# Clustered attention and routed experts on one core: the first expert turn's weight sums moved from VectorE to GpSimd, and its preparation placed at other steps

## The chip, the cores and the metric

The kernel runs on one core of a Trainium2 chip. The metric is the device time of one execution in microseconds. A core has five engines with a queue each: TensorE (PE; its weight loads are shown apart as PEld), VectorE (DVE), ScalarE (ACT), GpSimd (POOL) and SyncE (SP), which issues most of the transfers here. An engine works its queue in order; a semaphore holds an instruction until what it needs is there, and everything queued behind it waits too.

## The reference

Two blocks follow each other. The first is an attention in which a query sees only the keys of its own cluster:

```
q_assign = argmax(einsum('bhsd,hcd->bhsc', q_n, c_n))      # 16 clusters per head
k_assign = argmax(einsum('bhsd,hcd->bhsc', k_n, c_n))
mask     = q_assign[..., :, None] == k_assign[..., None, :]
scores   = where(mask, q @ k.T / sqrt(64), -1e9)
attn_out = softmax(scores) @ v                             # (4, 8, 768, 64)
```

Its output, as 3072 rows of 512, goes into a layer of 8 experts of which each row uses one:

```
logits     = x @ w_gate                                    # (3072, 8)
expert_idx = argmax(logits)
gate_w     = softmax(logits)[expert_idx]
y[rows of e] = relu(x[rows of e] @ w1[e]) @ w2[e]          # w1: 512x1024, w2: 1024x512
out        = gate_w * y
```

All is float32.

## The kernel before

**Attention.** The 32 heads (4 batches of 8) are worked as 16 pairs, numbered 0 to 15, four to a batch. A pair has two halves (h) of six key blocks (j). For each of the 12 steps TensorE computes scores of both heads into PSUM (L433: a float32 product of q and k, then a bf16 product of the masks mq and mk that pushes foreign clusters down), ScalarE takes the exponential (L445, tile A), and VectorE adds A into acc (L451), the softmax's denominators. After the 12 steps TensorE multiplies all A by v (L457), which takes about 8 us. The denominators of pair n are summed by TensorE early in pair n+1 (sum_up, L480, 12 products that need the last acc of pair n) and worked on by VectorE (weights_of, from L489).

**Preparation of a pair.** While pair n runs, pair n+1 is prepared: VectorE transposes q and k into qT and kT (L277), TensorE multiplies them by the centroids (L291), VectorE finds the best cluster (assign0 to assign2: L302, L309, L311, L318, L320, L322, and L327, which ends in ohT), and ScalarE scales the result into mk (L340) and mq (L337).

**Order of the work.** A list written out by hand says after which step each piece of other work is emitted: `at_pair(n, u, f)` puts f after step u of pair n, where u = 0 to 11 are the score steps, 12 is between the two halves of the product with v, and 13 is after it. `between(n, u)` (L868) calls what is listed. Each engine's queue follows from that list.

**Experts.** The rows are handled in ten turns, called slots. Slots 0 and 1 (288 rows each) take rows of the first three batches only, so that they can be prepared during the last batch, pairs 12 to 15; slot 0 is computed when attention has ended. The steps that prepare it:

- `number` (L598 to L607): VectorE computes each token's place and GpSimd writes the tokens to DRAM (tokens_of) by indirect transfers.
- `rank_first` (L642): 13 small VectorE instructions that pick the experts of slots 0 and 1 and write them, with offsets, to xe.
- `first_turns` (L849): SP loads the numbers from xe into registers (expert, places), fetches the token lists sf from DRAM (L712, L716), and then the expert's weights w1 (L97) and w2 (L105), 2048 KB each.
- `indices` (L722): VectorE turns sf into row numbers gi and si (L728, L729).
- `gather` (L731): GpSimd fetches the rows xg by indirect transfers (L738), three for a slot of 288 rows.
- `weigh` (L744): VectorE multiplies the rows by the softmax weights into xw (L755) and SP stores them in DRAM (turn_rows, L761).
- `take` (L765): SP loads them back as xs (L771) in the layout that VectorE's transpose needs.
- `turn_rows` (L776): VectorE transposes xs into xT (L780).
- `x_sums` (L791) and `w1_sums` (L809): the sums of one step of Strassen's scheme, four of xT's blocks (tile xc) and four of w1's (tiles a0 to a3, 128 x 1024 float32 each). Both are issued by `strassen` (L788), so they share line 789.

`layer1` (L947) then multiplies w1 and the rows with seven products per half instead of eight (L968). Its order of use for the weight sums is a2, a1, a0, a3. Between its products, hooks run the rest of pair 15: sum_up in hook 2, weights_of, gate and others behind it.

In w1_sums the sums depend on one another as follows:

```
0: lambda: (a21, a22, ALU.add), 1: lambda: (a22, A[2], ALU.subtract),
2: lambda: (a11, a21, ALU.subtract), 3: lambda: (a12, A[1], ALU.subtract),
```

Of the kernel before, what the change touches and what calls it, by code (L numbers as in the profile page):

```python
# [33 lines left out]
def kernel(  # L34
# [11 lines left out]
    nc = tc.nc  # L46
# [121 lines left out]
    with tc.manual_schedule(), ExitStack() as actx:  # L168
# [655 lines left out]
        def at_pair(n, u, f, *a):  # L824
            AT.setdefault((n, u), []).append(lambda: f(*a))
# [8 lines left out]
        for b in range(B - 1):  # L834
            n = HP * (b + 1)
# [8 lines left out]
            at_pair(n, 2, weights_of, n - 1)  # L844
        n = HP * (B - 1)
        slots = range(len(EARLY))
        at_pair(n + 1, 4, rank_first)

        def first_turns():  # L849
            for s in slots:  # L850
# [3 lines left out]
            GR[0]["w1"] = fetch1(GR[0]["e"], wa)  # L854
            GR[0]["w2"] = fetch2(GR[0]["e"], wa)

        at_pair(n + 1, 6, first_turns)
        for s in slots:
            at_pair(n + 1, 13, indices, s)
        at_pair(n + 2, 6, gather, 0)  # L860
        at_pair(n + 2, 13, weigh, 0)
        at_pair(n + 3, 1, take, 0)
        at_pair(n + 3, 4, turn_rows, 0)
        at_pair(n + 3, 6, x_sums, 0)
        at_pair(n + 3, 9, w1_sums, 0, (2, 1), nc.vector)
        at_pair(n + 3, 13, w1_sums, 0, (0, 3), nc.vector)

        def between(n, u):  # L868
            for f in AT.pop((n, u), ()):
# [24 lines left out]
    with tc.manual_schedule(), ExitStack() as ectx:  # L894
# [262 lines left out]
        n = NPAIR  # L1157
# [357 lines left out]
```

## Time and profile before

| | |
|---|---|
| runs | 660.57, 660.47, 659.32 us; median 660.47 |
| profiled execution | 659.27 us, of which the span from first to last instruction is 657.5 |
| granted TensorE clock | 0.998 |
| pair 13 (TensorE's first score to the next pair's) | 268.96 to 288.84, 19.88 us |
| pair 14 | 288.84 to 310.37, 21.53 us |
| pair 15 | 310.37 to 329.47, 19.10 us; no preparation of a next pair in it |
| slot 0, layer 1 | 329.47 to 347.20 |
| rank_first on VectorE | 279.60 to 281.86 |
| issue of w1 and w2 of slot 0 | 290.39 and 290.92; on their way 7.4 and 16.1 us |
| gathers on GpSimd (slot 0's three, slot 1's first) | start 293.49, 294.79, 296.83, 298.02 |
| slot 1's other two gathers | 311.75 and 313.09 |
| xw of slot 0 on VectorE | 310.36 to 313.63 |
| xT of slot 0 on VectorE | 322.41, after 2.48 us of waiting for xs |
| weight sums of slot 0 on VectorE | 329.26 to 331.75 and 333.59 to 335.95 |

In the profile's text a line has, in this order: source line, engine, operation, the tile written and the tiles read, size and number, then busy time and the mean of one instruction in ns, and at the end the idle time before and what ended it. A line in order of time starts with its start and its length in us; what stands in brackets is how long the engine stood idle before it and which instruction released it. A row of the table by stretch has start and end, its length, then busy us and number of instructions for PE, PEld, DVE, ACT and POOL, the granted clock, the share of the DMA engines that was busy, and GB/s. Times in all views count from the span's start.

### The profile page before, as it was taken

To read this page: it belongs to the slowest core of one execution; us is meant where nothing else is said; L and a number is where in the kernel's file an instruction comes from. 1 tells how busy PE (TensorE), PEld (TensorE's weight loads), DVE (VectorE), ACT (ScalarE), POOL (GpSimd) and SP (SyncE) were. 2 spreads that over 40 slices of the span, in tenths; PEclk is the share of its full clock that TensorE was granted. 3 is DMA by queue.
4 is the path that set the end of the run, shared out by engine and by line. 5 is a ranking of instruction groups with operands and counts; after the bars stand their busy time and mean duration, and the time that the engine had idled before them with its cause. 6 is when DMAs were issued, how large, how long until landed. Compare 5 with 4: busy or idle time off the path is not lost.

```text
span 657.5 us, 11491 instructions
## 1 busy us (share of the span) xinstructions
PE 644.2 (98%) x4252; PEld 423.3 (64%) x4252; DVE 490.0 (75%) x845; ACT 338.8 (52%) x584; POOL 130.8 (20%) x166
## 2 busy tenths in 40 slices
PE   8999999999999999999999999999999999999996
PEld 4444544455444454544484979989797987869773
DVE  6988888998889988989887997888869365572300
ACT  4677878768878777867532333333231331323210
POOL 4500000022000300041103522324240422140010
PEclk9999999999999999999999999999999999999999
DMA  7663455443355433347475587776684835614010
GB/s 150 150 120 68 76 94 97 72 80 68 73 97 98 74 76 72 72 132 227 117 273 156 187 314 264 252 275 211 249 307 170 273 138 165 233 74 173 7 49 19
DMA packets 189760, 95.38 MB, mean 145 GB/s; under 512 B 152895, under 2 KB 171839, under 8 KB 188416
## 3 DMA queue, kind: packets, MB, share of 16 engines
q1 hardware_dynamic: 184624, 81.56, 45.2%
q0 software_dynamic: 4928, 12.97, 6.1%
q8 instruction: 35, 0.57, 0.4%
q14 instruction: 29, 0.24, 0.1%
q10 hardware_dynamic: 144, 0.03, 0.0%
HBM read 74.10 MB, written 20.70 MB: 144 GB/s over the span
## 4 chain that ended last, share of the span: by engine, by line
PE 80%; issue 10%; DVE 5%; POOL 2%; ACT 1%; DMA 1%; POOLq 0%; DVEq 0%; ACTq 0%
PE sps L433 20%; PE mps L457 16%; PE bank L968 10%; PE sbank L968 8%; PE bank L1069 7%; PE bank L1088 7%; PE sbank L1069 6%; PE mps L480 2%; PE mps L291 1%; PE bank L937 1%; DMA xg<-x_rows,gi 1%; DVE xT L780 1%; POOL tokens_of L607 1%; DVE acc L451 1%; DVE a L789 1%
## 5 line engine op out<-in xcount | busy, mean ns | idle before, releaser
L445 ACT ACTIVATE A<-sps 128x768 f32<-128x768 f32 x192 | 152.1, 814 | 30.0 <-PE sps L433 29.4
L433 PE MATMUL sps<-qT,kT 64*128 64x384 f32 x768 | 158.9, 492 | 0.0
L451 DVE TENSOR_TENSOR acc<-acc,A 128x768 f32<-128x768 f32 x128 | 121.4, 948 | 11.4 <-ACT A L445 2.9
L457 PE MATMUL mps<-A,v_in 128*64 128x384 f32 x768 | 127.4, 488 | 0.0
L433 PEld LDWEIGHTS sps<-qT,kT 64*128 64x128 f32 x768 | 66.8, 187 | 52.2 <-issue 48.4
L457 PEld LDWEIGHTS mps<-A,v_in 128*64 128x64 f32 x768 | 53.7, 137 | 70.6 <-issue 62.9
L1043 POOL DMA_INDIRECT out_dram<-z,si x30 | 47.7, 1590 | 196.0 <-DVE z L926 167.2
L607 POOL DMA_INDIRECT tokens_of<-tg,pos_i x24 | 27.5, 1147 | 270.5 <-DVE pos_i L605 264.4
L433 PE MATMUL sps<-mq,mk 64*128 64x384 bf16 x384 | 64.9, 323 | 3.1 <-ACT mq L337 1.3
L1088 PE MATMUL bank<-w,h 128*128 128x512 f32 (+2 forms) x224 | 64.4, 596 | 0.0
L340 ACT ACTIVATE mk<-ohT,kscn,ksc 32x384 bf16<-32x384 bf16 x60 | 42.0, 700 | 40.5 <-DVE ohT L327 39.7
L968 PE MATMUL bank<-xT,w 128*128 128x144 f32 (+4 forms) x288 | 47.7, 309 | 0.0
L738 POOL DMA_INDIRECT xg<-x_rows,gi x30 | 38.4, 1280 | 47.0 <-DVE si L729 16.4
L968 PE MATMUL sbank<-xc,a 128*128 128x144 f32 (+4 forms) x288 | 47.7, 309 | 0.0
L1088 PEld LDWEIGHTS bank<-w,h 128*128 128x128 f32 (+2 forms) x224 | 24.6, 151 | 32.5 <-issue 32.3
L968 PEld LDWEIGHTS bank<-xT,w 128*128 128x128 f32 x288 | 43.8, 190 | 2.6 <-issue 2.2
L451 DVE TENSOR_TENSOR acc<-A 128x768 f32<-128x768 f32 x32 | 30.4, 952 | 19.2 <-ACT A L445 19.1
L968 PEld LDWEIGHTS sbank<-xc,a 128*128 128x128 f32 x288 | 43.4, 190 | 0.0
L926 DVE TENSOR_TENSOR h<-sbank,p 128x288 f32<-128x288 f32 (+4 forms) x18 | 9.2, 514 | 45.7 <-PE sbank L968 45.5
L433 PEld LDWEIGHTS <-mk 64*128 64x128 bf16 x384 | 19.9, 94 | 29.0 <-DVE mk L383 2.6
L986 ACT ACTIVATE h<-h 128x288 f32<-128x288 f32 (+4 forms) x36 | 17.6, 488 | 38.1 <-DVE h L926 38.1
L755 DVE TENSOR_TENSOR xw<-xg,sf 128x256 f32<-128x256 f32 (+2 forms) x60 | 32.8, 606 | 0.9 <-DMA xg<-x_rows,gi 0.6
(216 smaller groups left out, 900.5 us busy)
## 6 DMA issues: line engine op xcount, KB each, us to landing
w<-in_moe_w_dram SPq DMA_DIRECT2D x20, 2048.0 KB, 10.7
v_in<-in_v_dram SPq DMA_DIRECT2D x32, 192.0 KB, 2.5
x_rows<-x SPq DMA_DIRECT2D x64, 96.0 KB, 2.4
turn_rows<-xw SPq DMA_DIRECT2D x23, 256.0 KB, 2.0
q_in<-in_q_dram SPq DMA_DIRECT2D x60, 96.0 KB, 3.2
k_in<-in_k_dram SPq DMA_DIRECT2D x60, 96.0 KB, 3.2
xs<-turn_rows SPq DMA_DIRECT2D x16, 144.0 KB, 2.8
xs<-turn_rows SPq DMA_DIRECT2D x8, 208.0 KB, 4.2
```

Of the source, the lines that this page charges most:

```text
L340: nc.scalar.activation(dst, src, AF.Identity, bias=less, scale=big)
L433: nc.tensor.matmul(SP[n, h, j][:, a, 0:HS], lhsT=kt[rows, j * P : (j + 1) * P], rhs=qt[rows, h * HS : (h + 1) * HS], start=first, stop=not ...
L445: nc.scalar.activation(A[n, h, j], ps[:, :, 0:HS], AF.Exp, scale=D**-0.5)
L451: nc.vector.tensor_tensor(ACC[n, h], first, A[n, h, j], op=ALU.add)
L457: nc.tensor.matmul(O[n, h][D * a : D * (a + 1), 0:HS], lhsT=VIN[n][:, a, j, :], rhs=A[n, h, j][:, a, :], start=(j == 0), stop=(j == NQ - 1),)
L607: ins = nc.gpsimd.indirect_dma_start(out=t_d[:, :], out_offset=bass.IndirectOffsetOnAxis(ap=pos_i[:, i : i + 1], axis=0), in_=tg[:, b, i, ...
L738: nc.gpsimd.indirect_dma_start(out=xg[0:m], out_offset=None, in_=x_d[0:rows_in, :], in_offset=bass.IndirectOffsetOnAxis(ap=g["gi"][0:m, j ...
L755: nc.vector.tensor_tensor(xw[0:m, :, :, d2 * a : d2 * (a + 1)], xg[0:m].rearrange("p (r a d b) -> p a r b d", r=HP, a=2, b=DB)[:, a], g["s ...
L968: nc.tensor.matmul(ps[:, f * T2 : (f + 1) * T2], lhsT=w[:, k, (2 * j + f) * P : (2 * j + f + 1) * P], rhs=x[:, k, :], start=first and f + ...
L1043: ins = nc.gpsimd.indirect_dma_start(out=out[:, :], out_offset=bass.IndirectOffsetOnAxis(ap=GR[s]["si"][0:rows, j : j + 1], axis=0), in_=z ...
L1069: nc.tensor.matmul(ps[:, 0:H], lhsT=x[:, k, :], rhs=y[:, k, :], start=first and k == 0, stop=k == 3, skip_group_check=not first,)
L1088: nc.tensor.matmul(ps[i * m : (i + 1) * m, :], lhsT=h[:, f, j * P : j * P + m], rhs=w[:, f, :], start=(k == 0), stop=(k == FB // n - 1),)
```

## The change

Six entries of the hand-written list are changed, and the four weight sums of slot 0 go to another engine:

| step | before (pair, step) | after |
|---|---|---|
| rank_first | 13, 4 | 13, 9 |
| first_turns | 13, 6 | 13, 11 |
| indices of slots 0 and 1 | 13, 13 | 14, 2 |
| gather of slot 0 | 14, 6 | 14, 6 |
| weigh of slot 0 | 14, 13 | 14, 11 |
| take of slot 0 | 15, 1 | 14, 13 |
| turn_rows, x_sums of slot 0 | 15, 4 and 15, 6 | the same |
| w1_sums of slot 0 | 15, 9 and 15, 13 on VectorE | 14, 9 on GpSimd, all four |

In GpSimd's queue the four sums stand behind the three gathers of slot 0 and the first of slot 1, and ahead of the other two of slot 1. The first waits for w1; the second and the fourth wait for the sum before them. In SP's queue the order of the transfers stays as it was, and on VectorE only rank_first, indices and the sums change their places.

```diff
-        at_pair(n + 1, 4, rank_first)
+        at_pair(n + 1, 9, rank_first)
...
-        at_pair(n + 1, 6, first_turns)
+        at_pair(n + 1, 11, first_turns)
         for s in slots:
-            at_pair(n + 1, 13, indices, s)
+            at_pair(n + 2, 2, indices, s)
         at_pair(n + 2, 6, gather, 0)
-        at_pair(n + 2, 13, weigh, 0)
-        at_pair(n + 3, 1, take, 0)
+        at_pair(n + 2, 11, weigh, 0)
+        at_pair(n + 2, 13, take, 0)
         at_pair(n + 3, 4, turn_rows, 0)
         at_pair(n + 3, 6, x_sums, 0)
-        at_pair(n + 3, 9, w1_sums, 0, (2, 1), nc.vector)
-        at_pair(n + 3, 13, w1_sums, 0, (0, 3), nc.vector)
+
+        at_pair(n + 2, 9, w1_sums, 0, (2, 1, 0, 3), nc.gpsimd)
```

Here n is 12, the first pair of the last batch.

## The prediction

> **What bounds the kernel now.** I read the page first, then a table of busy time by stretch, then TensorE, VectorE and GpSimd in order of time around the turn from attention to experts. Of the page, three lines:
>
> ```profile
> PE 644.2 (98%) x4252; PEld 423.3 (64%) x4252; DVE 490.0 (75%) x845; ACT 338.8 (52%) x584; POOL 130.8 (20%) x166
> L445 ACT ACTIVATE A<-sps 128x768 f32<-128x768 f32 x192 | 152.1, 814 | 30.0 <-PE sps L433 29.4
> L451 DVE TENSOR_TENSOR acc<-acc,A 128x768 f32<-128x768 f32 x128 | 121.4, 948 | 11.4 <-ACT A L445 2.9
> ```
>
> TensorE is the bound: 13 us of 657.5 are left idle in all. A change to VectorE and GpSimd can only give back some of TensorE's idle time, or add to it. The averages (VectorE 75%) hide the stretch that counts. One row each for pairs 13, 14, 15 and layer 1 of the first turn (busy us of PE, PEld, DVE, ACT, POOL):
>
> ```profile
> 268.96:288.84 19.88, 19.88 (x156) 9.77 (x154) 18.21 (x45) 11.90 (x18) 6.77 (x6) 1.00 0.21 45
> 288.84:310.37 21.53, 20.21 (x154) 9.89 (x152) 19.49 (x37) 17.47 (x27) 4.58 (x4) 1.00 0.76 254
> 310.37:329.47 19.10, 19.10 (x146) 9.41 (x145) 15.88 (x27) 11.70 (x17) 2.26 (x2) 1.00 0.40 100
> 329.47:347.20 17.73, 16.76 (x144) 15.13 (x143) 14.69 (x37) 6.08 (x16) 2.04 (x3) 1.00 0.68 253
> ```
>
> TensorE idles 1.32 us in pair 14 and 0.97 us in layer 1, and VectorE is over 90% busy in pairs 13 and 14. TensorE in order of time names the waits:
>
> ```profile
> 290.86 0.32 PE L433 MATMUL sps<-mq,mk 64*128 64x384 bf16 x1 [1.10 <-ACT mq L337]
> 291.39 0.32 PE L433 MATMUL sps<-mq,mk 64*128 64x384 bf16 x1 [0.21 <-ACT mq L337]
> ...
> 338.75 1.25 PE L968 MATMUL sbank<-xT,a 128*128 128x144 f32 x8 [0.71 <-DVE h L926]
> ...
> 342.16 0.17 PE L592 MATMUL mps<-last,lt_b 128*128 128x8 bf16 x1 [0.21 <-DVE last L586]
> ```
>
> The masks mq came late since VectorE ran the 13 small instructions of rank_first (279.60 to 281.86, 2.2 us) ahead of pair 14's cluster assignment. The waits in layer 1 come from VectorE too, which was still at the weight sums:
>
> ```profile
> 329.26 1.22 DVE L789 TENSOR_TENSOR a<-w 128x1024 f32<-128x1024 f32 x1
> 330.52 1.23 DVE L789 TENSOR_TENSOR a<-w,a 128x1024 f32<-128x1024 f32 x1
> 331.66 2.01 DVE L451 TENSOR_TENSOR acc<-acc,A 128x768 f32<-128x768 f32 x2
> 333.59 1.22 DVE L789 TENSOR_TENSOR a<-w 128x1024 f32<-128x1024 f32 x1
> ```
>
> The last acc ends at 333.67. The 24 matmuls of L480 that need it run from 333.16 to 334.82, where they took 1.1 us in pair 15 (313.00 to 314.11): another 0.5 us that the releaser column doesn't show.
>
> [...] acc, ge, xw and the weight sums all have two SBUF inputs. [...]
>
> ```profile
> 366.40 2.35 DVE L789 TENSOR_TENSOR v<-w 128x1024 f32<-128x1024 f32 x2
> ...
> 366.69 2.92 POOL L738 DMA_INDIRECT xg<-x_rows,gi  x1 [3.18 <-DVE gi L728]
> ...
> 9.19 0.36 DVE L311 TENSOR_TENSOR ge<-sim,mx 128x192 bf16<-128x192 f32 x1
> ...
> 12.07 1.10 POOL L383 TENSOR_SCALAR mk<-ohT,ksc,kscn 32x192 bf16<-32x192 bf16 x2
> ...
> 12.87 0.51 DVE L311 TENSOR_TENSOR ge<-sim,mx 128x192 bf16<-128x192 f32 x1
> ```
>
> GpSimd's descriptor work, about 1 us elsewhere, took 2.92 us under two VectorE sums without a gap. And the same ge took 0.51 instead of 0.36 us while a GpSimd instruction, which ended at 13.17, was under way. [...]
>
> **The change, part by part.**
>
> *rank_first behind the assignment (u 4 to 9).* ohT of pair 14 then comes 2.2 us sooner (285.2), the masks are ready at 289.2 and needed at 289.7, so the 1.32 us of waits go. Next late is similar (L291), whose kT VectorE still ends at 293.1: its work up to there is only reordered. L291 would be reached 3.63 us after the pair's start, as in pair 13 (268.96 to 272.59), at 292.47. About 0.7 us of TensorE stall takes the old one's place; with the third mask's smaller lag gone too (the pair starts 288.84, and L291 ran at 294.25 for 292.47 unstalled, 1.78 late) the gain is 1.78 - 0.7 = 1.1 us.
>
> *first_turns (u 6 to 11), indices, gather.* The loads on SP waited for tokens_of before (sf issued at 287.49). Now rank_first ends at about 289.5; three register loads of about 0.75 us (the gap 288.49 to 289.28 between the two slots' sf issues) put sf at 291.7 and the last sf on its way at 294.1, landed at 295.8 (1.7 us). indices then stands at 296.5 on VectorE: 0.7 us to spare. w1 is issued at about 294.5, 4 us later, and with its 7.4 us to landing is there at 302. The order of SP's queue is unchanged: what stands behind w1 and w2, x_rows of pair 13, is not needed before pair 14's end. The four indirect DMAs start at 297 instead of 293.5 and land by about 309 (3.5 to 8.4 us before), weigh needs them at 309.4: tight, costed at nothing, up to 1 us if they are late. indices (0.6 us) moves in front of pair 14's VectorE work, so that VectorE is 1.0 us ahead of before there, not 1.6.
>
> *weigh and take (to u 11 and 13).* By the instruction order of both kernels nothing lies between old and new place on VectorE or SP: nothing.
>
> *The four sums leave VectorE.* 4 x 1.22 = 4.9 us off VectorE after 329; two of them (2.45 us) stood ahead of the last acc. Without other effects the last acc would end at 333.67 - 2.45 - 1.0 = 330.2, L480 would be reached at 333.16 - 1.1 = 332.1 and take 1.1 us: end 333.2, 1.6 us earlier. The 0.71 and 0.21 us behind it go as well, since weights_of and gate need not wait for the second pair of sums. Sum without contention: -1.6 - 0.9 = -2.5 us.
>
> *The four sums arrive on GpSimd.* In its queue they stand behind four gathers and wait for w1 (302); the second and fourth also wait for the one before. Queued behind them: the second and third gather of slot 1, which ran at 311.75 and 313.09 and whose rows weigh(1) reads at 342.0; with sums up to 316 or even 330 nobody waits. The price is on VectorE. From 302 on it is back to back, mostly with two-input instructions. Placed on before's rows less 1 us: the first sum gets in at top (a reduce, 303.7) and holds to 306.0, oh waits 1.7 us; the second gets in after oh and holds the first acc 1.7 us beyond ohT; the third and fourth get in at the 0.1 us gaps between acc's and cost 2.2 us each. Together about 7.7 us (9.2 less 1.5 under one-input work). Bounds: nothing, if GpSimd only fills the gaps; [...] some 10.5 us at 3 us a sum.
>
> *What that delays.* Pair 14's last acc ends at 317.3 instead of 309.5; L480 of pair 15 is reached at about 312.7, so TensorE stands for some 4.7 us. weigh, the stores and loads of turn_rows and xT follow at the old lag (xT 322.41 after xw 313.63), to 329.2. The last acc: 330.2 + 7.7 = 337.9, L480 ends at 338.9, +4.1 us on 334.82. Less the 0.9 us behind it: +3.2 us. From 347 on TensorE has nearly no gap, so the shift stays to the end.
>
> The profiled execution took 659.27 us (span 657.5 and 1.8 around it), so 662.5; it lies 1.2 us under the median shown, 660.47, and on that I forecast 663.6.
>
> **Rivals.** *A, VectorE has the right of way* and GpSimd fills the gaps: -2.5 us, 658.0. For it: no acc in the trace is longer than 0.995 us, though GpSimd read beside some. Against: those reads were short enough for the gaps, and the 0.51 us above. It decides if the sums delay VectorE little: 1.9 us (330.2 to 332.1) are free, and up to 3.1 us the kernel would still be 1.3 us faster. *B, GpSimd is starved*: as A, but the fourth sum ends after its use, which is at 338 (L968 sbank<-xT,a). It needs 9.2 us free of two-input work from 302 on; top, ohT, the transposes and the idle 2.48 us before xT give 7 by 322, so it would end near 330: no cost, within A. *C, half contention* (about 4 us): near nothing, 659.5 to 661.5.
>
> **How the numbers follow.** Contention with the delay worked out (661.3 to 667[...]): 0.55. A with B (657 to 659): 0.38. C: 0.07. A change under 0.2% (1.3 us) can't be told from none; so faster 0.38, same 0.07, slower 0.55. The likeliest case's own range is 661.3 to 667.0; eight in ten need the faster case as well, so 657.4 to 666.8.
>
> **What would show it.** Right: acc rows of 2 to 3.3 us near 303 to 318, L789 on POOL over 2.3 us, TensorE waiting for acc at L480 of pair 15, xT after 328. Wrong: acc's at 0.95 us throughout, pair 15 starting near 309.3 and lasting 19.1 us, layer 1 without the 0.71 us wait. The first part is right if no mq wait stands in pair 14 and one of about 0.7 us stands at L291; a VectorE wait for sf or xg would show the late loads.

## The result, and the profile after

Timed side by side on one chip, 14 executions of each kernel: before 659.24 us (657.98 to 662.15), after 662.78 us (660.69 to 666.99); ratio 1.0054, 95% interval 1.0034 to 1.0074. The change makes the kernel slower by about 3.5 us. The forecast was 3.1 us slower than the median it was made against (663.6 on 660.47).

The profiled execution of the changed kernel took 661.22 us (span 659.4, granted clock 0.995), only 1.95 us more than that of before. Where the rest of the 3.5 us comes from is one of the questions below.

The busy time by stretch (start and end, length, then busy us and instructions of PE, PEld, DVE, ACT and POOL, clock, DMA share, GB/s) of the changed kernel, for pair 14, pair 15 and layer 1:

```profile
289.22:309.49 20.27, 20.27 (x154) 9.78 (x152) 19.13 (x35) 11.50 (x17) 10.77 (x7) 1.00 0.69 247
309.49:333.66 24.17, 20.08 (x147) 9.73 (x145) 21.42 (x29) 15.51 (x23) 6.92 (x4) 1.00 0.43 99
333.66:349.82 16.16, 16.05 (x143) 15.14 (x142) 11.83 (x35) 6.08 (x16) 2.03 (x3) 1.00 0.75 278
```

Pair 14 is 1.26 us shorter than before, pair 15 is 5.07 us longer, layer 1 is 1.57 us shorter. With pair 14 starting 0.38 us later and 0.72 us gained after layer 1, this is +0.38 - 1.26 + 5.07 - 1.57 - 0.72 = +1.90 us of span. The first and the last of these terms are scatter between executions: with the same order of work up to there, pair 14 starts between 288.55 and 289.30 in the traces of e1, e3, e4 and e5, and in e5, which is this kernel again, 310.4 us follow layer 1, as before (310.3). From pair 14 to the end of layer 1 the loss is 2.24 us (2.12 in e5). No weight sum is left on VectorE, and yet it is busy for 21.42 us in pair 15, where it was 15.88. TensorE in order of time shows what pair 15 waits for:

```profile
309.49 0.92 PE L433 MATMUL sps<-qT,kT 64*128 64x384 f32 x4
313.06 0.32 PE L433 MATMUL sps<-mq,mk 64*128 64x384 bf16 x1 [2.65 <-ACT mq L337]
313.59 0.32 PE L433 MATMUL sps<-mq,mk 64*128 64x384 bf16 x1 [0.21 <-ACT mq L337]
...
317.20 0.68 PE L480 MATMUL mps<-acc,ones_s 128*32 128x192 f32 x10 [1.23 <-DVE acc L451]
...
337.35 0.92 PE L480 MATMUL mps<-acc,ones_s 128*32 128x192 f32 x16
338.53 1.25 PE L968 MATMUL bank<-xT,w 128*128 128x144 f32 x8
```

The idle time in layer 1 (0.71 and 0.21 us) is gone; new waits of 2.65, 0.21 and 1.23 us, 4.1 us in all, stand at the start of pair 15. The other 1.0 us of the 5.07 is not shown as idle: TensorE is shown busy for 20.08 us with the work that took 19.10. ScalarE is named for the first two, but it only passes on what VectorE's assignment gives it. VectorE in order of time, beside it GpSimd:

```profile
302.96 0.95 DVE L451 TENSOR_TENSOR acc<-A 128x768 f32<-128x768 f32 x1
303.83 2.52 DVE L318 TENSOR_TENSOR rank<-ge,first_cb 128x384 bf16<-128x384 bf16 x1
306.38 0.55 DVE L320 TENSOR_REDUCE top<-rank 128x24 bf16<-128x384 bf16 x1
306.97 2.02 DVE L322 TENSOR_TENSOR oh<-rank,top 128x384 bf16<-128x384 bf16 x1
309.02 0.58 DVE L327 STREAM_TRANSPOSE ohT<-oh 128x384 bf16<-128x384 bf16 x1
309.52 7.62 DVE L451 TENSOR_TENSOR acc<-acc,A 128x768 f32<-128x768 f32 x4
```

```profile
303.02 3.11 POOL L789 TENSOR_TENSOR a<-w 128x1024 f32<-128x1024 f32 x1 [0.82 <-DMA w<-in_moe_w_dram]
306.21 2.36 POOL L789 TENSOR_TENSOR a<-w,a 128x1024 f32<-128x1024 f32 x1
308.53 2.65 POOL L789 TENSOR_TENSOR a<-w 128x1024 f32<-128x1024 f32 x1
311.15 3.06 POOL L789 TENSOR_TENSOR a<-w,a 128x1024 f32<-128x1024 f32 x1
```

The two lists have to be read against each other. The first sum is shown from 303.02, under an acc that ends at 303.91, and it ends 2.22 us after that acc, at 306.13; rank, which took 0.35 us in this place before, then ends at 306.35. The second sum ends 2.22 us after rank, at 308.57. top has one input and isn't touched (0.55 us as before); oh, 0.56 us before, ends at 308.99. The third sum ends 2.19 us after oh, and the fourth 2.21 us after the first of the four acc's. The first two of the four acc's, by themselves:

```profile
309.52 2.48 DVE L451 TENSOR_TENSOR acc<-acc,A 128x768 f32<-128x768 f32 x1
312.11 2.91 DVE L451 TENSOR_TENSOR acc<-acc,A 128x768 f32<-128x768 f32 x1
```

They end 0.82 and 0.81 us after the third and the fourth sum. So there is one pattern: a blocked instruction of VectorE ends after the sum ahead of it by its usual length less about 0.13 us (0.22 us for rank, 0.42 for oh, 0.8 for an acc of 0.95), and a sum ends 2.2 us after the instruction of VectorE ahead of it, wherever either is shown to start. By these ends the two engines take turns: while the one works at such an instruction, the other's stands until it ends. rank lost 2.17 us, oh 1.46, the four acc's 3.5 (7.62 for 4.11): 7.1 us in all, while four sums of 1.22 us left VectorE.

### The profile page after: what moved, and what is told of

Same layout as the page of the kernel before. It is cut to its first block, busy times and chain, and to the rows that moved or that the text cites. A ratio compares the mean times of both kernels' runs of the same rounds, so it can differ in the third digit from the quotient of the medians.

```text
span 659.4 us, 11496 instructions
## 1 busy us (share of the span) xinstructions
PE 644.9 (98%) x4252; PEld 423.9 (64%) x4252; DVE 492.5 (75%) x841; ACT 339.0 (51%) x584; POOL 144.1 (22%) x170
## 4 chain that ended last, share of the span: by engine, by line
PE 81%; DVE 10%; DMA 3%; ACT 2%; issue 2%; SPq 1%; POOL 0%; POOLq 0%; DVEq 0%; ACTq 0%
PE sps L433 22%; PE mps L457 17%; PE bank L968 10%; PE sbank L968 8%; PE bank L1088 7%; PE bank L1069 6%; PE sbank L1069 5%; PE mps L480 3%; DMA w<-in_moe_w_dram 2%; PE mps L291 1%; DVE v L789 1%; DVE acc L451 1%; PE bank L937 1%; DVE xT L780 1%; DVE xw L755 1%
## 5 line engine op out<-in xcount | busy, mean ns | idle before, releaser
L445 ACT ACTIVATE A<-sps 128x768 f32<-128x768 f32 x192 | 152.3, 814 | 34.1 <-PE sps L433 33.5
L433 PE MATMUL sps<-qT,kT 64*128 64x384 f32 x768 | 160.6, 496 | 0.0
L451 DVE TENSOR_TENSOR acc<-acc,A 128x768 f32<-128x768 f32 x128 | 124.8, 975 | 11.8 <-ACT A L445 3.3
L738 POOL DMA_INDIRECT xg<-x_rows,gi x30 | 40.5, 1349 | 41.7 <-DVE si L729 17.2
L986 ACT ACTIVATE h<-h 128x288 f32<-128x288 f32 (+4 forms) x36 | 17.6, 488 | 37.3 <-DVE h L926 37.3
```

Of the source, the lines that this page charges most:

```text
L433: nc.tensor.matmul(SP[n, h, j][:, a, 0:HS], lhsT=kt[rows, j * P : (j + 1) * P], rhs=qt[rows, h * HS : (h + 1) * HS], start=first, stop=not ...
L445: nc.scalar.activation(A[n, h, j], ps[:, :, 0:HS], AF.Exp, scale=D**-0.5)
L451: nc.vector.tensor_tensor(ACC[n, h], first, A[n, h, j], op=ALU.add)
L738: nc.gpsimd.indirect_dma_start(out=xg[0:m], out_offset=None, in_=x_d[0:rows_in, :], in_offset=bass.IndirectOffsetOnAxis(ap=g["gi"][0:m, j ...
```

## The experiments

The theory was that a sum on GpSimd and a two-input instruction of VectorE stop each other to their ends, as in the two lists above, so that VectorE loses more than the 4.9 us it gives away; the trace of before has no sum on GpSimd that could have shown it. Against it stood: the later loads of the turn cause the loss; GpSimd's activity as such causes it; and, since the profiled execution shows just over half of the loss, something that the trace doesn't show. Each ratio is the kernel's time over that of before on the same chip.

**e1: the moved steps alone.** The sums are on VectorE in their old places.

```diff
-        at_pair(n + 2, 9, w1_sums, 0, (2, 1, 0, 3), nc.gpsimd)
+        at_pair(n + 3, 9, w1_sums, 0, (2, 1), nc.vector)
+        at_pair(n + 3, 13, w1_sums, 0, (0, 3), nc.vector)
```

> The steps moved as in the change, the four sums left on VectorE where they were. Contention theory (GpSimd's sums hold VectorE up, the moves by themselves help): no wait for mq in pair 14, TensorE about 1.2 us ahead at pair 15's start, the waits of layer 1 (0.71 and 0.21 us) still there, so about 1.0 to 1.3 us faster than before (ratio 0.998 to 0.9985). Rival (the moves hurt: w1, sf and the gathers are 4 us later, and VectorE waits for them): slower than before by 1 us or more, and most of the change's 3.5 us seen here.

659.56 us, 22 executions; ratio 0.9983 (0.9975 to 0.9992): faster by 1.1 us. TensorE in order of time has no wait for mq left in pair 14, and the waits in layer 1 as before:

```profile
289.58 0.33 PE L433 MATMUL sps<-mq,mk 64*128 64x384 bf16 x2
...
338.11 1.25 PE L968 MATMUL sbank<-xT,a 128*128 128x144 f32 x8 [0.72 <-DVE h L926]
```

With the sums on VectorE the later loads cost nothing that can be measured, and the moves give 1.1 us. The loss comes with the sums on GpSimd.

**e2: the sums alone.** The kernel before, with its own schedule.

```diff
-        at_pair(n + 3, 9, w1_sums, 0, (2, 1), nc.vector)
-        at_pair(n + 3, 13, w1_sums, 0, (0, 3), nc.vector)
+        at_pair(n + 2, 9, w1_sums, 0, (2, 1, 0, 3), nc.gpsimd)
```

> The sums on GpSimd at pair 14, step 9, every other step as before, so that w1 lands at 298 and not at 302. Contention theory: the sums run from about 299 to 311, VectorE loses about 7 us as in the change, pair 15's masks come 5 to 7 us late, and without the moves' gain the kernel is 4 to 5 us slower than before (ratio 1.006 to 1.008), so slower than the change itself. Rival (late loads): with the loads early the sums cost nothing, and the kernel is faster than before by about 1.5 us.

666.38 us, 4 executions; ratio 1.0087 (1.0072 to 1.0101), a little above what was expected: with the loads early again, the sums cost still more. TensorE in order of time:

```profile
310.55 0.92 PE L433 MATMUL sps<-qT,kT 64*128 64x384 f32 x4
316.62 1.01 PE L433 MATMUL sps<-mq,mk 64*128 64x384 bf16 x2 [5.16 <-ACT mq L337]
317.15 1.75 PE L433 MATMUL sps<-qT,kT 64*128 64x384 f32 x4
...
322.38 0.92 PE L433 MATMUL sps<-qT,kT 64*128 64x384 f32 x4
```

The wait is 5.16 us, and the same four products that took 0.92 us before it take 1.75 us behind it. The table by stretches of 4 us says why; the third number from the right is the granted clock:

```profile
310.00:314.00 4.00, 1.46 (x8) 0.36 (x5) 3.89 (x6) 0.78 (x2) 0.28 (x1) 1.00 0.00 0
314.00:318.00 4.00, 1.32 (x5) 0.78 (x7) 3.69 (x5) 3.90 (x7) 0.00 (x0) 0.63 0.00 0
318.00:322.00 4.00, 4.00 (x32) 2.06 (x32) 3.48 (x7) 3.25 (x6) 2.20 (x2) 0.52 0.53 156
322.00:326.00 4.00, 4.00 (x38) 2.20 (x32) 3.43 (x8) 2.44 (x4) 0.00 (x0) 1.00 0.50 155
```

While TensorE waited its clock was halved, and it stayed halved for some 5 us of work. In stretches of 2 us it is 1.00 up to 314, 0.76 from 314 to 316, 0.50 to 320, 0.54 to 322 and 1.00 behind that. If it fell in one step, this was near 315, some 3.5 us into the wait: an estimate from the 0.76. From the first mask product to the scores behind L480 TensorE took 5.76 us (316.62 to 322.38); the same products take 2.39 us up to L480 in the change and 1.11 us from there on in e1, so the halved clock cost about 2.3 us. The wait itself is longer than in the change, since w1 is there earlier: all four sums (299.19 to 310.28) hold up instructions ahead of pair 15's ohT (three acc's and ge) and cost 6.6 us there, where in the change only two sums do, at 3.6 us. The blocked instructions end as in the change, an acc 0.8 us and ge 0.4 us after the sum, a sum 2.2 us after VectorE.

**e3: GpSimd busy, but only writing.** Each sum is replaced by three fills of its tile; the weight sums of this turn are left out, and their tiles hold a constant.

```diff
+                A[i] = w1s.tile([P, 2, F // 2], F32, name=f"a{i}")
+                for _ in range(3):
+                    nc.gpsimd.memset(A[i], 0.02)
...
-        at_pair(n + 2, 9, w1_sums, 0, (2, 1, 0, 3), nc.gpsimd)
+        at_pair(n + 2, 9, w1_fill, 0, (2, 1, 0, 3))
```

> The changed kernel with each of the four sums on GpSimd replaced by three fills of its tile with a constant: GpSimd is as busy (about 12 us) but reads nothing from SBUF; the weight sums are left out, so the output is another. [...] VectorE's rows keep their usual length (acc 0.95 us), no wait at L480 or mq in pair 15, and the time is 2 to 2.5 us below before (ratio 0.996 to 0.997). Rival (GpSimd's place in the queue, its writes, or any work on it holds VectorE up): 2 to 4 us slower than before, as in the change.

656.67 us, 4 executions; ratio 0.9935 (0.9921 to 0.995). GpSimd and VectorE in order of time:

```profile
302.33 10.71 POOL L827 MEMSET a<- 128x1024 f32 x11
```

```profile
303.45 0.35 DVE L318 TENSOR_TENSOR rank<-ge,first_cb 128x384 bf16<-128x384 bf16 x1
...
305.51 4.11 DVE L451 TENSOR_TENSOR acc<-acc,A 128x768 f32<-128x768 f32 x4
```

GpSimd is as busy as in the change, 10.7 us at the same place, and VectorE loses nothing: rank 0.35, four acc's 4.11, as before. So neither GpSimd's activity nor its writes do the harm; what the sums have and the fills have not is the reading (and the adding, which these runs don't take apart from it). The profiled execution is 656.78 us, 2.5 us under that of before: the sum without contention that the prediction worked out. The median is 4.0 us under that of before, more than the 2 to 2.5 us expected, and no run shows why. Between this and the change's profiled execution lie 4.4 us.

**e5: the change again,** on another chip.

> The changed kernel itself once more, beside the next two. Gate theory (GpSimd's sums make TensorE wait at pair 15's start, and in some executions that wait lets its clock fall to half for a few us): executions with a mean clock of 0.995 and more lie at 1.5 to 2.5 us above the kernel before, those at 0.994 and less 3 to 7 us above, median near 1.005. Rival (the scatter has nothing to do with the clock): times and clocks don't go together.

662.72 us, 9 executions; ratio 1.005 (1.0029 to 1.0072). The waits in the profile are those of the first run (2.58 us for mq, 1.23 us for acc), and the profiled execution, 661.94 us, again lies in the faster half. Over all executions, each kernel's number with a mean clock under 0.994 (this limit was set after the runs; the expected one, 0.994 or less, would count 15 of the change's 23, 2 of the 22 of e6, and 2 of the 117 of before):

| kernel | executions | of them under 0.994 | longest wait for mq at pair 15 |
|---|---|---|---|
| before, in three sets | 117 | 0 | none |
| the change (first run and e5) | 23 | 11 | 2.65 us |
| e2 | 4 | 4 | 5.16 us |
| e1, e3, e4, e7 to e10 | 101 | 0 | 1.65 us or less |

The 11 have a median of 663.9 us, the other 12 of 661.4 us. A mean lower by 0.003 over 660 us is 4 us at the half clock of e2's trace, or 2 us lost: about that difference, as an estimate. The mean holds something else too: the profiled execution of the change has a clock of 0.83 between 10 and 20 us, that of before 1.00, and this alone takes 0.003 off. The 0.995 in the profile of the change is this; from 20 to 640 us its clock is 1.00. Under 0.994 an execution has lost more than that, but one with a halved clock in pair 15 and a full one at the start can't be told by its mean, and times follow the mean only loosely (664.92 and 665.35 us at 0.994). A trace of the changed kernel with the halved clock in pair 15 was not caught.

**e6: TensorE kept busy during the wait.** Thirty small products go into the next score's tile, which that score then overwrites.

```diff
-            if first:
+            if first and (n, h, j) not in SP:
...
+            if (n, h, j) == (NPAIR - 1, 0, 0):
+                SP[n, h, 1] = ps_s.tile([P, 2, 512], F32, name="sps")
+                for _ in range(30):
+                    nc.tensor.matmul(SP[n, h, 1][:, 0, 0:P], lhsT=ones_b, rhs=lt_b, start=True, stop=True)
```

> The changed kernel with 30 small bf16 products of constants (128 columns each, some 2.5 us in all, into a score tile that is overwritten next) ahead of the first mask product of pair 15, so that TensorE works while it waits for mq. They add work and take no wait away. Gate theory: the clock stays at 0.995 or more, the time falls to 1 to 2.5 us above the kernel before (ratio 1.002 to 1.004) and scatters less. Rival (only the wait for VectorE costs): the same median as the changed kernel or more (1.005 to 1.007).

661.01 us, 22 executions; ratio 1.0026 (1.0015 to 1.0036), against e5's 1.005 (1.0029 to 1.0072) on the same chip. TensorE in order of time (the added lines shift the later line numbers by four; L445 is now the added product):

```profile
310.56 1.85 PE L445 MATMUL sps<-lt_b,ones_b 128*128 128x128 bf16 x30
313.12 0.32 PE L433 MATMUL sps<-mq,mk 64*128 64x384 bf16 x1 [0.72 <-ACT mq L337]
...
317.28 0.68 PE L484 MATMUL mps<-acc,ones_s 128*32 128x192 f32 x10 [1.24 <-DVE acc L455]
```

The first mask product comes at the same time as in the change, so the path is no shorter; TensorE has more to do, and the median is 1.7 us lower. One of 22 executions is under 0.994, where the change had 11 of 23. The two intervals overlap a little (1.0029 to 1.0036); the count of low clocks is the stronger sign. So a halved clock behind the waits is the likely part of the loss that the profiled execution doesn't show; that it sits there in the changed kernel is argued from the counts, from this run and from e2's trace.

**e7: the sums on GpSimd in pieces.** Each sum is four instructions of 256 columns.

```diff
+                for b, c in ((0, 0), (0, 1), (1, 0), (1, 1)) if eng is nc.gpsimd else ():
+                    r = slice(F // 4 * c, F // 4 * (c + 1))
+                    strassen(eng, A[i][:, b, r], x[:, b, r], y[:, b, r], op)
+                if eng is nc.gpsimd:
+                    continue
```

> The changed kernel with each GpSimd sum in four pieces of 256 columns, 16 instructions in place of 4, about 0.6 us each. [...] VectorE's longest acc falls from 2.91 to about 1.6 us, the sums take longer on GpSimd (over 13 us), and VectorE's loss stays 5 to 8 us, since the reads are as many; the time is about that of the change. [...]

657.86 us, 20 executions; ratio 0.9968 (0.9958 to 0.9978): faster than before, which was not expected. Grouped by tile between 300 and 320 us (number, shortest/median/longest in ns, first and last start), the pieces and the acc's beside them:

```profile
L789 POOL TENSOR_TENSOR a<-w,a x8: 726/1441/1504, 306.0 to 319.7; 128x256 f32<-128x256 f32 x8
```

```profile
L451 DVE TENSOR_TENSOR acc<-acc,A x6: 917/1296/1306, 299.5 to 317.9; 128x768 f32<-128x768 f32 x6
L451 DVE TENSOR_TENSOR acc<-A x2: 952/1187/1422, 302.0 to 316.3; 128x768 f32<-128x768 f32 x2
```

A piece alone takes 0.73 us; beside acc's it takes twice that (1.44 us), and the acc's some 0.3 us more (1.30 for 0.95). The two engines take turns, piece and acc, about 1.4 us for each round, and nobody waits long. VectorE and TensorE in order of time:

```profile
302.88 0.89 DVE L318 TENSOR_TENSOR rank<-ge,first_cb 128x384 bf16<-128x384 bf16 x1
...
304.39 1.06 DVE L322 TENSOR_TENSOR oh<-rank,top 128x384 bf16<-128x384 bf16 x1
305.49 0.58 DVE L327 STREAM_TRANSPOSE ohT<-oh 128x384 bf16<-128x384 bf16 x1
305.99 5.12 DVE L451 TENSOR_TENSOR acc<-acc,A 128x768 f32<-128x768 f32 x4
311.04 5.37 DVE L755 TENSOR_TENSOR xw<-xg,sf 128x256 f32<-128x256 f32 x6
...
323.67 1.33 DVE L780 STREAM_TRANSPOSE xT<-xs 128x1152 f32<-128x1152 f32 x1
```

```profile
310.06 0.32 PE L433 MATMUL sps<-mq,mk 64*128 64x384 bf16 x1 [0.15 <-ACT mq L337]
```

VectorE's loss is not gone: rank 0.54, oh 0.50, four acc's 1.0, six xw's 2.1 (5.37 for 3.27) and two acc's 0.8 make 4.9 us. But ohT ends at 306.1 instead of 309.6, so TensorE waits 0.15 us and not 2.65, and half of the loss falls into the 2.48 us that VectorE spent waiting for xs before: here xT starts without a wait. The sums need 17.6 us of GpSimd (302.8 to 320.5) instead of 11.2, and nobody waits for GpSimd there.

**e8: in two pieces of 512 columns.** As e7 with `for b, c in ((0, 0), (1, 0))` and `r = slice(0, F // 2)`.

> The changed kernel with each GpSimd sum in two pieces of 512 columns. If one piece is held to its end and what counts is how long VectorE waits at a time, it lies between the whole sums (ratio 1.005) and the quarters (0.997): longest acc 2.0 us, a wait for mq in pair 15 of about 1 us, 0.998 to 1.003. Rival (the gain of the quarters came from something else, such as another order in GpSimd's queue): as the quarters, 0.996 to 0.998.

661.29 us, 20 executions; ratio 1.0013 (1.0006 to 1.0021). With the change, e7 and e7's kernel once more (e10, below) it makes a row:

| columns of one GpSimd instruction | longest acc, 300 to 320 us | longest wait for mq | ratio |
|---|---|---|---|
| 1024 (the change) | 2.91 us | 2.65 us | 1.0054 (1.0034 to 1.0074) |
| 512 (e8) | 2.04 us | 1.65 us | 1.0013 (1.0006 to 1.0021) |
| 256 (e7) | 1.42 us | 0.15 us | 0.9968 (0.9958 to 0.9978) |
| 256 (e10) | 1.48 us | 0.89 us | 0.9965 (0.9956 to 0.9974) |

In these four, the shorter the instruction, the shorter the longest hold: an acc of usually 0.95 us takes 2.91, 2.04, and 1.42 or 1.48 us. So an acc was held to the end of one GpSimd instruction and got its turn before the next. All of these kernels read the same bytes on GpSimd.

**e4: VectorE's own idle places.** The moves of the change, and the sums on VectorE: two where it waits for xs, two after its last acc.

```diff
+        at_pair(n + 3, 4, w1_sums, 0, (2, 1), nc.vector)
         at_pair(n + 3, 4, turn_rows, 0)
...
-        at_pair(n + 2, 9, w1_sums, 0, (2, 1, 0, 3), nc.gpsimd)
+        at_pair(n + 3, 13, w1_sums, 0, (0, 3), nc.vector)
```

> The moves, with the sums on VectorE but elsewhere: two ahead of the transpose of xs in pair 15, where VectorE waited 2.48 us for its transfer, two after the last acc, where it waits for TensorE's L480. If VectorE's order alone was the cause of the waits in layer 1, all gains come without GpSimd: no mq wait in pair 14, last acc near 330.2, no 0.71 us wait in layer 1, 2.0 to 2.5 us faster than before (ratio 0.996 to 0.997). Rival (the waits in layer 1 have another cause, or the idle time moves with the sums): as the moves alone, 1.0 to 1.3 us faster.

657.81 us, 6 executions; ratio 0.9956 (0.9942 to 0.997). VectorE in order of time:

```profile
318.45 1.18 DVE L789 TENSOR_TENSOR a<-w 128x1024 f32<-128x1024 f32 x1
319.67 1.23 DVE L789 TENSOR_TENSOR a<-w,a 128x1024 f32<-128x1024 f32 x1
321.89 1.38 DVE L780 STREAM_TRANSPOSE xT<-xs 128x1152 f32<-128x1152 f32 x1 [1.00 <-DMA xs<-turn_rows]
```

Two sums of 2.4 us fit ahead of xT, which still waits 1.00 us for xs and starts at 321.89 (322.41 before). No second engine is needed.

**e9 and e10: e4 and e7 side by side** on one chip, which was another.

> The sums on VectorE in its idle places once more, beside the quarters on GpSimd: the same as in its first run, 0.9945 to 0.997, and 0 to 1 us faster than the quarters, whose last acc comes about 2 us later. Rival: no difference that can be told.

> The quarters on GpSimd once more, for comparison on the same chip: 0.996 to 0.998, with its last acc about 0.5 us after TensorE could use it. Rival: its first result was chance, and it lies at 1.0 or more.

e9: 658.57 us, 9 executions, ratio 0.9968 (0.9958 to 0.9978). e10: 658.45 us, 20 executions, ratio 0.9965 (0.9956 to 0.9974). Both are faster than before and than the change, and no difference between them can be told. In its second profile e7's kernel waited 0.89 us for mq, so its 0.15 us is not a fixed figure.

## Why the prediction was right, and where its sizes were off

*rank_first behind the assignment: right.* Predicted 1.1 us; pair 14 became 1.26 us shorter, and e1 was 1.1 us faster. The wait of 0.7 us that was to stand at L291 isn't shown as one, but it is there: the products of qT start at 292.85 and those of kT at 293.36, which started together before (294.25 and 294.27), so L291 came 1.78 us sooner after the pair's start and gave 0.5 us of that back.

*The loads: right on the whole.* indices waited 0.52 us for the token lists, where 0.7 us to spare had been reckoned, so that VectorE was 0.43 us ahead of before at rank (303.83 for 304.26) and not 1.0; and the first sum started at 303.02 for 302 since w1 was later. e1 shows that this costs nothing that can be told as long as the sums are on VectorE.

*weigh and take: nothing, as said.* No run took them alone; e1 holds them with the rest.

*The sums leave VectorE: right.* Predicted -2.5 us without contention; e3's profiled execution has -2.5 (656.78 on 659.27); its median has -4.0 in four executions (0.9935), which stays open. The waits in layer 1 went, as predicted.

*The sums on GpSimd: the hold and its total right, the distribution not.* That a sum and a two-input instruction stop each other to the end, and how long a sum takes on GpSimd, the trace of before, without a sum on GpSimd, had not shown; the step assumed both. Measured since: rank held to 2.52 us for 0.35, no conflict with a fill (e3: rank 0.35, four acc's 4.11 us), none with the one-input top (0.55 us as before), a sum of 2.36 us at the shortest, and 7.1 us of loss, where 7.7 had been worked out. The total hardly hangs on which instructions are blocked, since each sum holds up one of them. The prediction let the first sum wait for an instruction with one input, top, so that only oh came late, ohT at about 307.1. The sums did not wait for that: this one got in at the boundary between acc and rank, and e2's and e10's first ones at one between two-input instructions too (an acc of 1.48 us in e10). So rank and oh were both held, for 3.6 us instead of 1.7, with VectorE 0.6 us less ahead, and ohT ended at 309.60.

*What that delays: the step that was mis-sized.* The prediction had 4.7 us of waiting at L480 and left out the wait for mq. Measured: 2.65 + 0.21 us for mq and 1.23 for acc, 4.1 us, and pair 15 longer by 5.07. The place had been missed since ohT had been taken as 2.5 us too early. The end of this step was near: xT at 328.32 (329.2 predicted), L480's end at 338.5 (338.9). From pair 14 to the end of layer 1 2.24 us were lost, where 3.2 were worked out; the profiled execution as a whole lost 1.95 us.

*A term was missing: the halved clock.* A wait of TensorE was costed at its length; in e2 the first 5 us of work behind one of 5.16 us ran at 0.50 to 0.54. The 11 of 23 executions with a low mean clock have a median 2.5 us higher, and e5 and e6 speak for a halved clock as the cause, though no trace of the changed kernel holds it in pair 15. The median of +3.5 us is thus near the forecast of +3.1 us partly by luck: two errors offset each other, since the loss in one execution was taken 1.0 to 1.2 us too large, and this term was not there.

*The rivals.* A (right of way for VectorE) falls with rank at 2.52 us, B with the sums' end at 314.2, long before their use. C (about 4 us of contention) is not this kernel; e7 comes near it with 4.9 us, and lies lower than C's time since that loss falls beside VectorE's idle time.

## What to carry to other kernels

Work given to GpSimd was not free here for a VectorE that was full of two-input instructions: 4.9 us taken off cost 7.1 us, each sum on GpSimd stopping the next instruction with two inputs until it ended (rank 2.52 us for 0.35, an acc up to 2.91 for 0.95). Look first for idle places in VectorE's own queue, for which a table of its waits is enough (e4); if the work must go, cut it into short instructions, so that no long hold falls on a chain that TensorE waits for (e7: no acc over 1.42 us, and 0.15 us of waiting for mq where there were 2.65). And cost a new TensorE wait of the size seen here (2.65 us and more) at more than its length, since the clock may be halved behind it: seen at 5.16 us (0.50 to 0.54), likely at 2.65.

## What was not expected of the hardware

- Two-input instructions of VectorE and sums on GpSimd took turns at every boundary, even where VectorE's instructions followed without a gap: in the traces of the change and of e2 no sum was kept waiting by more than one instruction (it ended 2.2 us behind it), and no instruction by more than one sum (an acc ended 0.8 us behind it).
- Pieces of 256 columns (0.73 us alone, 1.44 us under contention) and acc's (0.95 us alone, mostly 1.30) took turns so evenly that the kernel became faster than before (0.9968), although the sums took 6 us longer (17.6 for 11.2).
- A 5.16 us wait of TensorE brought some 5 us at half clock behind it (0.50 to 0.54 up to 322; four products 1.75 for 0.92 us); with waits of 2.65 and 0.21 us close together, 11 of 23 executions show a low mean clock, with 1.65 us or less none of 101.
- Thirty useless products of 62 ns each in a wait made the median 1.7 us lower.
